# Highway output of a cross-covariance attention kernel written as T*max(h,0) - (T-1)*x

## The chip, the cores and the metric

The kernel runs on one core of a Trainium2 chip. The metric is the device time of one execution in microseconds (us), lower is better. Before the change the median of three runs is 414.38 us (414.25 to 415.24).

## What is computed

The inputs q, k and v have the shape (4, 6336, 256) in float32. The first half is a cross-covariance attention over channels, and its output x feeds a highway layer:

```python
qn = q / (norm(q, axis=1) + 1e-06)          # norm over the 6336 rows
kn = k / (norm(k, axis=1) + 1e-06)
a  = softmax(kn.T @ qn / tau)               # 256 x 256 per batch
x  = (v @ a).reshape(25344, 256)
H  = maximum(x @ w_h, 0)
T  = 1 / (1 + exp(-(x @ w_t + b_t)))
out = T * H + (1 - T) * x
```

## The kernel before

The four batches are worked one after another, and each has three stages. A row block has 128 rows (a subtile); a batch has 50 of them, the last with 64 rows, in groups of 16, 16, 16 and 2.

**Stage A** (L120 to L149) reads q and k and accumulates, over the 50 subtiles, six matmuls each into two PSUM banks (`sg`): k against q, and the two diagonal blocks that give the norms. **The middle** (L151 to L248) turns these into the softmax matrix `a`, transposes it (`at`), and multiplies it with w_h and w_t on TensorE. Its result `mr` holds three matrices side by side: `a` itself (columns 0 to C), a@w_h (C to 2C) and a@w_t (2C to 3C). So one pass over v gives x, h and the argument of the gate.

**Stage B** (L254 on) goes over the rows of v in pairs of subtiles, 24 full pairs and two single subtiles for each batch. For a pair, `emit_transpose` (L268) makes four matmuls against the identity into `vtps` (one PSUM buffer) and casts the result to f16 in SBUF as `vtsb` (four buffers). The cast is done by VectorE (DVE, L296) for even pairs and by ScalarE (ACT, L301) for odd ones. Transposes are written two pairs ahead (LOOKAHEAD). Then, for each subtile u of the pair, five matmuls follow in this order: `p3b` (L329), `p3a` (L336), `p3b`, `p3a`, and the bias into `p3b` (L343). A `p3a` bank holds x in columns 0 to C and h in columns C to 2C for one subtile, and there are three such banks. A `p3b` bank holds the gate's argument for both subtiles of a pair, and there are two.

The output of a pair is then made in five steps. ACT computes uu = sigmoid(-z) = 1 - T from `p3b` (L354) for the pair. For each subtile ACT computes hh = relu(h) from `p3a` (L366), and DVE computes dd = hh - x with x read from `p3a` (L370). GpSimd (POOL) computes pp = uu * dd for the pair (L378). DVE computes o = hh - pp into the output stage (L382). A `p3a` bank is free for TensorE when hh and dd of its subtile are done. The tiles uu, hh, dd and pp have four buffers each.

Loads of q, k and v are issued by POOL's queue (L401, L408), stores by the sync engine's queue (L418, L425), one store per 8 subtiles. A framework puts the instructions of each engine in an order, allots buffers and sets the waits; each engine then works strictly in that order.

Of the kernel before, what the change touches and what calls it, by code (L numbers as in the profile page):

```python
# [9 lines left out]
AluOp = mybir.AluOpType  # L10
Act = mybir.ActivationFunctionType
f32 = mybir.dt.float32
# [3 lines left out]
P = 128  # L16
# [3 lines left out]
def kernel(  # L20
# [11 lines left out]
    nc = tc.nc  # L32

    B, N, C = q.shape
# [7 lines left out]
    def rows_of(s):  # L42
        return last_rows if s == nsub - 1 else P
# [5 lines left out]
    while s < nsub:  # L49
# [7 lines left out]
    small_pool = ctx.enter_context(tc.tile_pool(name="small", bufs=4))  # L57
# [14 lines left out]
        out=wht[:, :, 0:C], in_=moe_w_h.rearrange("(kt jl) m -> jl kt m", kt=2)  # L72
    )
    nc.gpsimd.dma_start(
        out=wht[:, :, C : 2 * C], in_=moe_w_t.rearrange("(kt jl) m -> jl kt m", kt=2)
# [26 lines left out]
    def load_v(bb, gi):  # L102
        s0, ns = groups[gi]
        vt = stream_pool.tile([P, ns, C], f16, tag="v_in", bufs=3,
                              name=f"v{bb}_{gi}")
        _load_group(nc, vt, v[bb], s0, ns, rows_of)
        v_tiles[(bb, gi)] = vt
# [4 lines left out]
    for b in range(B):  # L112
# [7 lines left out]
        for gi, (s0, ns) in enumerate(groups):  # L120
            qt = q_tiles.pop((b, gi))
            kt_ = k_tiles.pop((b, gi))
            for si in range(ns):
                s_idx = s0 + si
                nr = rows_of(s_idx)
# [33 lines left out]
        for idx, (c, off) in enumerate(  # L159
# [3 lines left out]
                out=junk[:, idx, :],  # L163
                in0=ssb[:, c, off : off + P],
                scalar=0.0,
                in1=ident0,
                op0=AluOp.bypass,
                op1=AluOp.mult,
# [8 lines left out]
        for c in range(2):  # L177
            nc.vector.tensor_scalar(
                out=dcat[:, c, :],
                in0=ident0,  # L180
                scalar1=inv[:, 2 + c : 3 + c],
                scalar2=inv_tau,
                op0=AluOp.mult,
                op1=AluOp.mult,
# [7 lines left out]
        for c in range(2):  # L192
            nc.vector.scalar_tensor_tensor(
                out=t1[:, c, :],
                in0=ssb[:, c, 0:C],
                scalar=inv[:, c : c + 1],
                in1=cqbs,
                op0=AluOp.mult,
                op1=AluOp.mult,
# [5 lines left out]
            out=rs, in_=araw, axis=mybir.AxisListType.X, op=AluOp.add  # L205
# [3 lines left out]
        for c in range(2):  # L209
            nc.vector.tensor_scalar(  # L210
                out=mr[:, c, 0:C],
                in0=araw[:, c, :],
                scalar1=rinv[:, c : c + 1],
                scalar2=None,
                op0=AluOp.mult,
                op1=AluOp.bypass,
# [15 lines left out]
        for jk in range(2):  # L232
            nc.scalar.copy(
                out=at_sb[:, jk, :].rearrange("p (ic i) -> p ic i", ic=2),
                in_=atps[:, :, jk, :],
# [19 lines left out]
        for gi, (s0, ns) in enumerate(groups):  # L255
            si = 0
            while si < ns:
                pn = min(2, ns - si)
                if pn == 2 and rows_of(s0 + si) != rows_of(s0 + si + 1):
                    pn = 1  # L260
# [7 lines left out]
        def emit_transpose(pi):  # L268
            gi, s0, si, pn, nrows = pairs[pi]
            if si == 0:  # L270
                if gi + 1 < len(groups):
                    load_v(b, gi + 1)
                ostg_tiles[gi] = stream_pool.tile(
                    [P, groups[gi][1], C], f32, tag="o_out", name=f"o{b}_{gi}"
                )
            vt_in = v_tiles[(b, gi)]
            vtps = psum_pool.tile(
                [P, 2, 2, P], f32, tag="vtps", name=f"vtps{b}_{gi}_{si}"
            )
            pcnt = 0  # L280
            for u in range(pn):
                nr = nrows[u]
                for c in range(2):
                    nc.tensor.matmul(  # L284
                        vtps[:, u, c, 0:nr],
                        vt_in[0:nr, si + u, bass.ts(c, P)],
                        ident[0:nr, 0:nr],
                        start=(pcnt == 0),
                        stop=(pcnt == 2 * pn - 1),
                    )  # L290
                    pcnt += 1
            vt_sb = work_pool.tile(
                [P, 2, 2, P], f16, tag="vtsb", bufs=4, name=f"vtsb{b}_{gi}_{si}"
            )
            if pi % 2 == 0:
                nc.vector.tensor_copy(  # L296
                    out=vt_sb[:, 0:pn, :, 0 : nrows[0]],
                    in_=vtps[:, 0:pn, :, 0 : nrows[0]],
                )
            else:  # L300
                nc.scalar.copy(  # L301
                    out=vt_sb[:, 0:pn, :, 0 : nrows[0]],
                    in_=vtps[:, 0:pn, :, 0 : nrows[0]],
                )
            vtsb_tiles[pi] = vt_sb

        for pi in range(min(LOOKAHEAD, len(pairs))):
            emit_transpose(pi)

        for pi in range(len(pairs)):  # L310
            if pi + LOOKAHEAD < len(pairs):
                emit_transpose(pi + LOOKAHEAD)
            gi, s0, si, pn, nrows = pairs[pi]
            vt_sb = vtsb_tiles.pop(pi)
            ostg = ostg_tiles[gi]
            ns = groups[gi][1]
            p3b = psum_pool.tile(
                [P, 2, C], f32, tag="p3b", bufs=2, name=f"p3b_{b}_{gi}_{si}"
            )
            p3a = []  # L320
            for u in range(pn):
                nr = nrows[u]
                pa = psum_pool.tile(
                    [P, 2 * C], f32, tag="p3a", bufs=3,
                    name=f"p3a_{b}_{s0 + si + u}",
                )
                p3a.append(pa)
                for kt in range(2):
                    nc.tensor.matmul(  # L329
                        p3b[0:nr, u, :],  # L330
                        vt_sb[:, u, kt, 0:nr],
                        mr[:, kt, 2 * C : 3 * C],
                        start=(kt == 0 and u == 0),
                        stop=False,
                    )
                    nc.tensor.matmul(  # L336
                        pa[0:nr, :],
                        vt_sb[:, u, kt, 0:nr],
                        mr[:, kt, 0 : 2 * C],
                        start=(kt == 0),  # L340
                        stop=(kt == 1),
                    )
                nc.tensor.matmul(  # L343
                    p3b[0:nr, u, :],
                    ident[:, 0:nr],
                    btb,
                    start=False,
                    stop=(u == pn - 1),
                )

            nr0 = nrows[0]
            uu = small_pool.tile([P, 2, C], f32, tag="uu",
                                 name=f"uu{b}_{gi}_{si}")
            nc.scalar.activation(  # L354
                out=uu[0:nr0, 0:pn, :],
                in_=p3b[0:nr0, 0:pn, :],
                func=Act.Sigmoid,
                scale=-1.0,
            )
            hh = small_pool.tile([P, 2, C], f32, tag="hh",  # L360
                                 name=f"hh{b}_{gi}_{si}")
            dd = small_pool.tile([P, 2, C], f32, tag="dd",
                                 name=f"dd{b}_{gi}_{si}")
            for u in range(pn):
                nr = nrows[u]
                nc.scalar.activation(  # L366
                    out=hh[0:nr, u, :], in_=p3a[u][0:nr, C : 2 * C],
                    func=Act.Relu,
                )
                nc.vector.tensor_tensor(  # L370
                    out=dd[0:nr, u, :],
                    in0=hh[0:nr, u, :],
                    in1=p3a[u][0:nr, 0:C],
                    op=AluOp.subtract,
                )
            pp = small_pool.tile([P, 2, C], f32, tag="pp",
                                 name=f"pp{b}_{gi}_{si}")
            nc.gpsimd.tensor_tensor(  # L378
                out=pp[0:nr0, 0:pn, :], in0=uu[0:nr0, 0:pn, :],
                in1=dd[0:nr0, 0:pn, :], op=AluOp.mult,  # L380
            )
            nc.vector.tensor_tensor(  # L382
                out=ostg[0:nr0, si : si + pn, :], in0=hh[0:nr0, 0:pn, :],
                in1=pp[0:nr0, 0:pn, :], op=AluOp.subtract,
            )


            if si + pn >= ns:
                o0 = 0
                while o0 < ns:  # L390
                    on = min(OGS, ns - o0)
                    _store_group(nc, ob, ostg, s0, o0, on, rows_of)
                    o0 += on
                del ostg_tiles[gi]
                v_tiles.pop((b, gi))
# [36 lines left out]
_INS = ['q', 'k', 'v', 'tau', 'moe_w_h', 'moe_w_t', 'moe_b_t']  # L432
_OUTS = [((25344, 256), 'float32')]
#: Inputs that are plain numbers.
_NUMBERS = {'tau': 1.0}


# [26 lines left out]
```

## Time and profile before

| | |
|---|---|
| median of three runs | 414.38 us (414.25 to 415.24) |
| span of the profiled execution, first to last instruction | 412.4 us |
| TensorE (PE) matmul busy | 297.5 us, 72% |
| DVE busy | 208.9 us, 51% |
| ACT busy | 183.3 us, 44% |
| POOL busy | 189.2 us, 46% |
| chain that ended last, by engine | PE 24%, DMA 24%, DVE 23%, POOL 17%, issue 7%, ACT 4% |

The profile gives no other time for the profiled execution than its span; 2.0 us lie between that span and the median. The engines' shares are averages over the stages, and no engine is near 100%. The chain of waits is followed back from the last instruction, so its shares tell which work the end waited for. Busy times of matmuls overlap each other, so spacing between starts, not the sum of durations, tells what TensorE can do.

### The profile page before, as it was taken

The numbers are of one execution on the slowest core, as the hardware profiler recorded it, in microseconds if no ns is written. First come the engines' busy times: TensorE is split into PE (matmuls) and PEld (weight loads), VectorE is DVE, ScalarE is ACT, GpSimd is POOL, SyncE is SP. The second block draws the span as 40 slices with busy tenths as digits, with TensorE's granted clock in tenths as the row PEclk, the third lists the DMA queues.
The fourth block names the chain that finished last, engine by engine and source line by source line (L and its number), as shares of the span: only waits on it lengthen the run. The fifth ranks groups of instructions, "written<-read, shape, count | busy, mean of one in ns | idle before, by whom it ended". The sixth has DMA issues, their size and how long they took to land.

```text
span 412.4 us, 6770 instructions
## 1 busy us (share of the span) xinstructions
PE 297.5 (72%) x2637; PEld 212.1 (51%) x2637; DVE 208.9 (51%) x426; ACT 183.3 (44%) x407; POOL 189.2 (46%) x173
## 2 busy tenths in 40 slices
PE   0186839809877899968777999777778938776770
PEld 0176737506544698544445986444447815444440
DVE  0000103707876704497767232887766144786663
ACT  1000126605655306756555055566552166655561
POOL 9212322634646634555548441557366002754453
PEclk9999969957999999999999999999999968999996
DMA  7999999999962999999439999494329700433333
GB/s 95 198 199 197 198 198 199 197 233 188 195 193 70 217 245 198 197 222 241 124 103 173 238 205 198 94 209 138 109 67 215 163 0 0 113 102 103 103 102 121
DMA packets 103456, 65.57 MB, mean 159 GB/s; under 512 B 1537, under 2 KB 103425, under 8 KB 103425
## 3 DMA queue, kind: packets, MB, share of 16 engines
q0 software_dynamic: 77568, 39.20, 70.3%
q1 hardware_dynamic: 25856, 25.95, 20.6%
q8 instruction: 20, 0.33, 0.3%
q14 instruction: 12, 0.09, 0.1%
HBM read 78.38 MB, written 25.95 MB: 253 GB/s over the span
## 4 chain that ended last, share of the span: by engine, by line
PE 24%; DMA 24%; DVE 23%; POOL 17%; issue 7%; ACT 4%; POOLq 0%; DVEq 0%; ACTq 0%
POOL pp L378 15%; DVE o L382 14%; DMA k<-in_k_dram 14%; DVE dd L370 7%; PE p3a L336 7%; DMA v<-in_v_dram 6%; PE sg L129 5%; DMA q<-in_q_dram 4%; PE p3b L329 3%; PE sg L136 2%; PE sg L143 2%; PE vtps L284 2%; ACT hh L366 2%; PE p3b L343 1%; DVE vtsb L296 1%
## 5 line engine op out<-in xcount | busy, mean ns | idle before, releaser
L378 POOL TENSOR_TENSOR pp<-uu,dd 128x512 f32<-128x512 f32 (+1 forms) x104 | 131.4, 1273 | 144.0 <-DVE dd L370 64.8
L336 PE MATMUL p3a<-mr,vtsb 128*128 128x512 f16 (+1 forms) x400 | 134.7, 385 | 33.6 <-DVE dd L370 33.5
L382 DVE TENSOR_TENSOR o<-hh,pp 128x512 f32<-128x512 f32 (+1 forms) x104 | 94.4, 923 | 52.3 <-POOL pp L378 52.3
L366 ACT ACTIVATE hh<-p3a 128x256 f32<-128x256 f32 x200 | 76.1, 386 | 87.1 <-PE p3a L336 57.5
L129 PE MATMUL sg<-q,k 128*128 128x256 f16 (+1 forms) x400 | 94.7, 281 | 25.0 <-DMA k<-in_k_dram 24.1
L329 PE MATMUL p3b<-mr,vtsb 128*128 128x256 f16 (+1 forms) x400 | 100.3, 276 | 0.6 <-ACT uu L354 0.5
L370 DVE TENSOR_TENSOR dd<-hh,p3a 128x256 f32<-128x256 f32 x200 | 75.4, 413 | 29.2 <-ACT hh L366 29.0
L136 PE MATMUL sg<-k 128*128 128x128 f16 (+1 forms) x400 | 89.8, 225 | 0.0
L143 PE MATMUL sg<-q 128*128 128x128 f16 (+1 forms) x400 | 89.7, 224 | 0.0
L296 DVE CAST vtsb<-vtps 128x512 f16<-128x512 f32 (+1 forms) x52 | 34.5, 664 | 98.4 <-PE vtps L284 98.1
L284 PE MATMUL vtps<-ident,v 128*128 128x128 f16 (+1 forms) x400 | 41.1, 222 | 34.9 <-DVE vtsb L296 22.7
L336 PEld LDWEIGHTS <-vtsb 128*128 128x128 f16 (+1 forms) x400 | 39.3, 99 | 42.4 <-issue 18.9
L329 PEld LDWEIGHTS <-vtsb 128*128 128x128 f16 (+1 forms) x400 | 39.3, 99 | 42.2 <-issue 26.7
L354 ACT ACTIVATE uu<-p3b 128x512 f32<-128x512 f32 (+1 forms) x104 | 59.8, 579 | 0.1
L284 PEld LDWEIGHTS <-v 128*128 128x128 f16 (+1 forms) x400 | 30.8, 99 | 54.2 <-issue 32.6
L129 PEld LDWEIGHTS <-k 128*128 128x128 f16 (+1 forms) x400 | 40.2, 100 | 30.5 <-DMA k<-in_k_dram 29.9
L343 PE MATMUL p3b<-btb,ident 128*128 128x256 f16 x200 | 55.2, 276 | 0.0
L143 PEld LDWEIGHTS <-q 128*128 128x128 f16 (+1 forms) x400 | 40.2, 101 | 6.9 <-issue 1.1
L301 ACT CAST vtsb<-vtps 128x512 f16<-128x512 f32 (+1 forms) x52 | 29.3, 563 | 29.2 <-PE vtps L284 29.2
L153 ACT COPY ssb<-sg 128x512 f32<-128x512 f32 x8 | 4.3, 589 | 84.7 <-PE sg L143 84.7
L136 PEld LDWEIGHTS <-k 128*128 128x128 f16 (+1 forms) x400 | 40.2, 101 | 1.7 <-issue 1.4
L401 POOL DMA_DIRECT2D k<-in_k_dram x12 | 14.1, 1176 | 27.9 <-PE sg L143 23.5
(44 smaller groups left out, 123.2 us busy)
## 6 DMA issues: line engine op xcount, KB each, us to landing
out_dram<-o SPq DMA_DIRECT2D x24, 1024.0 KB, 5.4
q<-in_q_dram POOLq DMA_DIRECT2D x12, 1024.0 KB, 19.6
k<-in_k_dram POOLq DMA_DIRECT2D x12, 1024.0 KB, 17.4
v<-in_v_dram POOLq DMA_DIRECT2D x12, 1024.0 KB, 18.0
out_dram<-o SPq DMA_DIRECT2D x4, 128.0 KB, 9.6
q<-in_q_dram POOLq DMA_DIRECT2D x4, 64.0 KB, 23.1
k<-in_k_dram POOLq DMA_DIRECT2D x4, 64.0 KB, 22.6
v<-in_v_dram POOLq DMA_DIRECT2D x4, 64.0 KB, 4.5
```

What stands on the lines that cost most here:

```text
L129: nc.tensor.matmul(sg[c][:, 0:C], kt_[0:nr, si, bass.ts(c, P)], qt[0:nr, si, :], start=first, stop=False,)
L136: nc.tensor.matmul(sg[c][:, C : C + P], kt_[0:nr, si, bass.ts(c, P)], kt_[0:nr, si, bass.ts(c, P)], start=False, stop=False,)
L143: nc.tensor.matmul(sg[c][:, C + P : C + 2 * P], qt[0:nr, si, bass.ts(c, P)], qt[0:nr, si, bass.ts(c, P)], start=False, stop=last,)
L284: nc.tensor.matmul(vtps[:, u, c, 0:nr], vt_in[0:nr, si + u, bass.ts(c, P)], ident[0:nr, 0:nr], start=(pcnt == 0), stop=(pcnt == 2 * pn - 1),)
L329: nc.tensor.matmul(p3b[0:nr, u, :], vt_sb[:, u, kt, 0:nr], mr[:, kt, 2 * C : 3 * C], start=(kt == 0 and u == 0), stop=False,)
L336: nc.tensor.matmul(pa[0:nr, :], vt_sb[:, u, kt, 0:nr], mr[:, kt, 0 : 2 * C], start=(kt == 0), stop=(kt == 1),)
L343: nc.tensor.matmul(p3b[0:nr, u, :], ident[:, 0:nr], btb, start=False, stop=(u == pn - 1),)
L354: nc.scalar.activation(out=uu[0:nr0, 0:pn, :], in_=p3b[0:nr0, 0:pn, :], func=Act.Sigmoid, scale=-1.0,)
L366: nc.scalar.activation(out=hh[0:nr, u, :], in_=p3a[u][0:nr, C : 2 * C], func=Act.Relu,)
L370: nc.vector.tensor_tensor(out=dd[0:nr, u, :], in0=hh[0:nr, u, :], in1=p3a[u][0:nr, 0:C], op=AluOp.subtract,)
L378: nc.gpsimd.tensor_tensor(out=pp[0:nr0, 0:pn, :], in0=uu[0:nr0, 0:pn, :], in1=dd[0:nr0, 0:pn, :], op=AluOp.mult,)
L382: nc.vector.tensor_tensor(out=ostg[0:nr0, si : si + pn, :], in0=hh[0:nr0, 0:pn, :], in1=pp[0:nr0, 0:pn, :], op=AluOp.subtract,)
```

## The change

The gate is kept as T (`tt`, sigmoid without the sign). DVE makes two products per subtile with one instruction each: th = max(h, 0) * T and ux = (T - 1) * x, each reading one operand from the `p3a` bank and one from `tt`. POOL subtracts them into the output stage. ACT's relu, DVE's difference dd, POOL's product and DVE's final subtraction go. The cast of the transposed v goes to DVE for every fourth pair instead of every second.

```diff
-            if pi % 2 == 0:
+            if pi % 4 == 0:
                 nc.vector.tensor_copy(out=vt_sb[...], in_=vtps[...])
...
             nc.scalar.activation(
-                out=uu[0:nr0, 0:pn, :],
+                out=tt[0:nr0, 0:pn, :],
                 in_=p3b[0:nr0, 0:pn, :],
                 func=Act.Sigmoid,
-                scale=-1.0,
             )
             for u in range(pn):
                 nr = nrows[u]
-                nc.scalar.activation(
-                    out=hh[0:nr, u, :], in_=p3a[u][0:nr, C : 2 * C],
-                    func=Act.Relu,
-                )
-                nc.vector.tensor_tensor(
-                    out=dd[0:nr, u, :],
-                    in0=hh[0:nr, u, :],
-                    in1=p3a[u][0:nr, 0:C],
-                    op=AluOp.subtract,
-                )
-            nc.gpsimd.tensor_tensor(
-                out=pp[0:nr0, 0:pn, :], in0=uu[0:nr0, 0:pn, :],
-                in1=dd[0:nr0, 0:pn, :], op=AluOp.mult,
-            )
-            nc.vector.tensor_tensor(
-                out=ostg[0:nr0, si : si + pn, :], in0=hh[0:nr0, 0:pn, :],
-                in1=pp[0:nr0, 0:pn, :], op=AluOp.subtract,
-            )
+                nc.vector.scalar_tensor_tensor(
+                    out=th[0:nr, u, :],
+                    in0=p3a[u][0:nr, C : 2 * C],
+                    scalar=0.0,
+                    in1=tt[0:nr, u, :],
+                    op0=AluOp.max,
+                    op1=AluOp.mult,
+                )
+                nc.vector.scalar_tensor_tensor(
+                    out=ux[0:nr, u, :],
+                    in0=tt[0:nr, u, :],
+                    scalar=1.0,
+                    in1=p3a[u][0:nr, 0:C],
+                    op0=AluOp.subtract,
+                    op1=AluOp.mult,
+                )
+            nc.gpsimd.tensor_tensor(
+                out=ostg[0:nr0, si : si + pn, :], in0=th[0:nr0, 0:pn, :],
+                in1=ux[0:nr0, 0:pn, :], op=AluOp.subtract,
+            )
```

## Rows read from the trace of the kernel before

**Rows 1.** Span and mean granted TensorE clock of the core.
```profile
core 0: 412.4 us, clock 0.950
```

**Rows 2.** Stretches of 10 us: length, busy us by engine (count), granted clock, DMA share, GB/s.
```profile
80.00:90.00 10.00, 1.14 (x8) 0.51 (x7) 2.88 (x7) 1.57 (x4) 4.72 (x4) 0.70 1.34 230
...
380.00:390.00 10.00, 7.43 (x56) 4.78 (x56) 6.09 (x14) 5.81 (x13) 5.06 (x4) 1.00 0.32 108
```

**Rows 3.** Chain of waits, 383 to 389 us: start us, us, what.
```profile
383.15 1.27 POOL pp L378
384.45 0.69 DVE o L382
...
388.00 0.39 ACT hh L366
388.42 1.28 POOL pp L378
```

**Rows 4.** Timeline of POOL: pair 7 and pair 24 of batch 0, pairs 1 and 24 after.
```profile
96.93 1.58 POOL L378 TENSOR_TENSOR pp<-uu,dd 128x512 f32<-128x512 f32 x1 [11.01 <-ACT uu L354]
...
138.55 3.77 POOL L378 TENSOR_TENSOR pp<-uu,dd 128x512 f32<-128x512 f32 x3 [1.37 <-DVE dd L370]
...
169.26 1.27 POOL L378 TENSOR_TENSOR pp<-uu,dd 128x512 f32<-128x512 f32 x1 [2.76 <-ACT uu L354]
...
225.34 3.77 POOL L378 TENSOR_TENSOR pp<-uu,dd 128x512 f32<-128x512 f32 x3 [1.36 <-DVE dd L370]
...
256.22 1.26 POOL L378 TENSOR_TENSOR pp<-uu,dd 128x512 f32<-128x512 f32 x1 [11.82 <-ACT uu L354]
...
313.29 3.77 POOL L378 TENSOR_TENSOR pp<-uu,dd 128x512 f32<-128x512 f32 x3 [1.36 <-DVE dd L370]
...
345.41 1.26 POOL L378 TENSOR_TENSOR pp<-uu,dd 128x512 f32<-128x512 f32 x1 [28.35 <-ACT uu L354]
...
403.89 1.94 POOL L378 TENSOR_TENSOR pp<-uu,dd 128x512 f32<-128x512 f32 x2 [1.20 <-DVE dd L370]
```

**Rows 5.** Timeline of all engines, 385 to 389 us.
```profile
385.06 1.07 DVE L370 TENSOR_TENSOR dd<-hh,p3a 128x256 f32<-128x256 f32 x3
...
385.52 0.38 PE L336 MATMUL p3a<-mr,vtsb 128*128 128x512 f16 x1 [0.61 <-DVE dd L370]
...
386.06 0.27 PE L343 MATMUL p3b<-btb,ident 128*128 128x256 f16 x1
386.17 0.39 PE L284 MATMUL vtps<-ident,v 128*128 128x128 f16 x4
...
386.39 0.27 PE L329 MATMUL p3b<-mr,vtsb 128*128 128x256 f16 x1
...
387.86 0.41 DVE L370 TENSOR_TENSOR dd<-hh,p3a 128x256 f32<-128x256 f32 x1
...
388.19 0.68 DVE L296 CAST vtsb<-vtps 128x512 f16<-128x512 f32 x1
```

**Rows 6.** Timeline at the start of stage B, batch 3, ACT and DVE.
```profile
341.97 0.38 ACT L366 ACTIVATE hh<-p3a 128x256 f32<-128x256 f32 x1 [1.33 <-PE p3a L336]
...
342.39 0.42 DVE L370 TENSOR_TENSOR dd<-hh,p3a 128x256 f32<-128x256 f32 x1 [5.18 <-ACT hh L366]
```

**Rows 7.** Groups by line and shape: busy us, mean ns, idle before.
```profile
L354 ACT ACTIVATE uu<-p3b 128x512 f32<-128x512 f32 x96 | 56.8, 596 | 0.1
...
L301 ACT CAST vtsb<-vtps 128x512 f16<-128x512 f32 x48 | 28.2, 588 | 29.0 <-PE vtps L284 29.0
...
L162 DVE SCALAR_TENSOR_TENSOR junk<-ssb,ident 128x128 f32<-128x128 f32 x16 | 3.7, 285 | 0.0
L193 DVE SCALAR_TENSOR_TENSOR t<-ssb,inv,cqbs 128x256 f32<-128x256 f32 x8 | 3.5, 481 | 2.6 <-ACT cqbs L189 2.6
```

**Rows 8.** Instructions by tile (dd, o), 340 to 400 us: duration ns, min/median/max.
```profile
L370 DVE TENSOR_TENSOR dd<-hh,p3a x45: 404/414/422, 342.4 to 399.1; 128x256 f32<-128x256 f32 x45
L382 DVE TENSOR_TENSOR o<-hh,pp x21: 673/693/1740, 346.7 to 397.8; 128x512 f32<-128x512 f32 x21
```

More of the change, by code (lines that the diff above doesn't have):

```diff
@@ L351 @@
             nr0 = nrows[0]
-            uu = small_pool.tile([P, 2, C], f32, tag="uu",
-                                 name=f"uu{b}_{gi}_{si}")
+            tt = small_pool.tile([P, 2, C], f32, tag="tt",
+                                 name=f"tt{b}_{gi}_{si}")
             nc.scalar.activation(
-                out=uu[0:nr0, 0:pn, :],
+                out=tt[0:nr0, 0:pn, :],
                 in_=p3b[0:nr0, 0:pn, :],
                 func=Act.Sigmoid,
-                scale=-1.0,
             )
-            hh = small_pool.tile([P, 2, C], f32, tag="hh",
-                                 name=f"hh{b}_{gi}_{si}")
@@ L362 @@
-            dd = small_pool.tile([P, 2, C], f32, tag="dd",
-                                 name=f"dd{b}_{gi}_{si}")
+            th = small_pool.tile([P, 2, C], f32, tag="th",
+                                 name=f"th{b}_{gi}_{si}")
+            ux = small_pool.tile([P, 2, C], f32, tag="ux",
+                                 name=f"ux{b}_{gi}_{si}")
             for u in range(pn):
                 nr = nrows[u]
-                nc.scalar.activation(
-                    out=hh[0:nr, u, :], in_=p3a[u][0:nr, C : 2 * C],
-                    func=Act.Relu,
-                )
-                nc.vector.tensor_tensor(
-                    out=dd[0:nr, u, :],
-                    in0=hh[0:nr, u, :],
+                nc.vector.scalar_tensor_tensor(
[5 more added lines that the diff above has]
+                    op1=AluOp.mult,
+                )
+                nc.vector.scalar_tensor_tensor(
+                    out=ux[0:nr, u, :],
+                    in0=tt[0:nr, u, :],
+                    scalar=1.0,
@@ L373 @@
                     in1=p3a[u][0:nr, 0:C],
-                    op=AluOp.subtract,
-                )
-            pp = small_pool.tile([P, 2, C], f32, tag="pp",
-                                 name=f"pp{b}_{gi}_{si}")
+                    op0=AluOp.subtract,
+                    op1=AluOp.mult,
+                )
             nc.gpsimd.tensor_tensor(
-                out=pp[0:nr0, 0:pn, :], in0=uu[0:nr0, 0:pn, :],
-                in1=dd[0:nr0, 0:pn, :], op=AluOp.mult,
-            )
-            nc.vector.tensor_tensor(
-                out=ostg[0:nr0, si : si + pn, :], in0=hh[0:nr0, 0:pn, :],
-                in1=pp[0:nr0, 0:pn, :], op=AluOp.subtract,
+                out=ostg[0:nr0, si : si + pn, :], in0=th[0:nr0, 0:pn, :],
```

## Prediction

> **What bounds the kernel now.** I read the spans first, then the stretches of 10 us, then the chain of waits, then the timeline inside one period of it. The span is 412.4 us at a mean granted clock of 0.950 [rows 1]. The stretches show two regimes. Up to about 93 us the transfers hold the kernel: from 80 to 90 us TensorE works 1.14 us of 10 while the DMA moves 230 GB/s. In the regime behind it, from 380 to 390 us, no engine is full (TensorE 7.43, DVE 6.09, ACT 5.81, POOL 5.06 of 10), the DMA moves 108 GB/s, and the clock is at its upper level of 2.4 GHz [rows 2]. So stage B waits on itself there: it is a loop of latencies, and not an engine, that sets its pace.
>
> The chain shows the loop. From one pp on the chain to the next it is 388.42 - 383.15 = 5.27 us, and it advances two pairs [rows 3]. The reader is to see the order: POOL multiplies for 1.27 us, DVE's o comes 0.03 us behind it and lasts 0.69, the dd of the next pair stands behind o in DVE's queue, and only that dd frees the p3a bank for which TensorE waits (0.61 us idle, released by dd) [rows 5]. TensorE then works until ACT's hh at 388.00, and hh ends just ahead of the next pp [rows 3]. So POOL's product and DVE's last subtraction, 1.27 and 0.69 us, hold TensorE up once in two pairs because they are ahead of dd in DVE's queue.
>
> The pace over whole batches comes from the pp of the first and the 24th pair of each batch (pair 7 to 24 in batch 0, behind the stall for v). It is 41.62, 56.08, 57.07 and 58.48 us [rows 4], 213.25 us in all for 17 + 3 x 23 = 86 intervals: **2.48 us per pair**. What lies outside (stage A, the middle, the start up to 96.93 us) holds nothing that the change edits, except for the first six pairs of batch 0, which run ahead of a transfer anyway. I take it as unchanged.
>
> **The change, part by part.** *Removed from ACT:* two relus per pair. *Moved to ACT:* a cast of 0.59 us for every fourth pair [rows 7]. ACT was not the bound and ends with less work: free. *POOL:* one 128x512 operation of two SBUF operands stays one such operation, 1.27 us [rows 4]; a subtraction for a product, between the same price and nothing known otherwise, and I take the same. Its place changes: nothing on DVE waits for it any more, only the store does, and the buffers of th and ux (four pairs deep). Cover: 1.27 us of work, and now and then a load's issue, in a period over 2.2 us.
>
> *DVE:* dd twice and o once go, four products come. The o goes with its long cases, where it starts under POOL's product and lasts up to 1740 instead of 693 ns. The products have one operand in PSUM and one in SBUF, as dd has, and dd never lasts over 422 ns, beside POOL or not [rows 8]. The price of scalar_tensor_tensor with a PSUM operand is in no row. From below: dd, 0.41 us, with the next instruction 0.33 us behind its start (387.86 to 388.19) [rows 5]. From above: the same operation at 128x256, 0.481 us, but with its scalar read from a tile. The row nearest to it is L162, the same operation with its scalar in the instruction: 0.285 us at 128 columns [rows 7]. From 256 to 512 columns a DVE operation of this kind grows from 0.414 to 0.693 us [rows 8], 0.14 us per 128 columns, so 0.285 + 0.14 = **0.42 us**, next start after 0.34. DVE's work per pair is at most 4 x 0.42 + 0.68/4 = 1.85 us, below the period.
>
> *The wait that the change adds:* th needs T, and T needs the whole pair's p3b, whose last matmul is the bias of the second subtile. Before, the first subtile's bank needed only its own p3a, hh and dd. With three banks, the second subtile of pair n+1 takes the bank of the first subtile of pair n. That closes a new loop, worked out from one release of p3a to the next:
>
> - p3a granted to the start of the bias matmul: 385.52 to 386.06, 0.54 us; the bias itself 0.27 [rows 5]
> - TensorE to ACT: 0.05, an estimate from the other two handovers
> - sigmoid over the pair: 0.60 [rows 7]
> - ACT to DVE: 341.97 + 0.38 to 342.39, 0.04 [rows 6]
> - th of the first subtile to the start of ux: 0.34; ux: 0.42
> - DVE to TensorE: 385.06 + 0.41 to 385.52, 0.05 [rows 5]
>
> The sum is 2.31 us. Beside it TensorE needs, per pair, two subtiles of 0.54 + 0.11 + 0.11 = 0.76 and 0.22 for the transposes (386.17 to 386.39) [rows 5], 1.74 us: it hides in the loop. Queued behind th and ux on DVE are the second subtile's two products and every fourth cast. The second bank comes free 2 x 0.34 us later, 1.0 us ahead of the next round: free. The cast on DVE (0.68 us [rows 5]) can come between. Its transposes are issued at 0.65, right behind the bias, and last 0.39, so it would run from 1.09 to 1.77, while th could start at 1.50; 0.27 on one pair in four is 0.07. **New period: 2.38 us.**
>
> The gain is 86 x (2.48 - 2.38) = 8.6 us. At the end of the run DVE's last subtraction goes but POOL's queue of three operations stays; I count nothing. 412.4 - 8.6 = 403.8 us of span; with the 2.0 us between span and median, **405.8 us**. The unknown prices give the ends of this case: no cast in the way and DVE at 0.41 and 0.33 makes 2.29 us and a gain of 16.3 (398); products half the way to the dearer row below (0.45, next start after 0.37) make 2.44 us and leave 3.4 (411). The change trades a loop of 2.48 us for another of nearly that length, so large sums of removed work (two relus, an o) matter little.
>
> **The rivals.**
>
> *1. The products are dearer, and nothing changes.* With 0.481 us and 0.40 to the next start the loop is 2.31 + 0.06 + 0.06 + 0.07 = 2.50, the time 416; in between lies no change. For it: the only 128x256 row of this operation [rows 7]. Against it: the surplus goes well with the scalar read from a tile, which the new ones don't have. The Trainium skill (VectorE: DVE Perf Modes, sections "The DRAIN you can't avoid" and "Rules for kernel authors") speaks against the change here: VectorE flushes its pipe behind each operation, so one is to keep the number of operations low, and the same section lets an operation that isn't held start earlier. Taken strictly, ux would start a full 0.42 behind th, which makes 2.46 us and 413; the row with a start 0.33 behind a start [rows 5] says otherwise.
>
> *2. Slower: an order that puts something between the bias and th.* The engines work in a fixed order that I can't see for the changed kernel. ACT now casts three pairs in four. If such a cast stands ahead of the sigmoid and starts just before it is due, the loop pays up to 0.59 [rows 7] on three pairs of four, 0.44: 2.31 + 0.44 = 2.75, 86 x 0.27 = 23 us more, 438. The same comes about if the cast on DVE stands behind the four products and TensorE's next transposes wait for it in the one vtps buffer. It decides from 0.17 us per pair on (2.48 - 2.31). For it: casts and transposes wait for each other already, in the one buffer. Against it: the transposes stand between pairs [rows 5], so that their cast falls due after the sigmoid.
>
> *3. Faster: the stalls are filled.* TensorE has 2.38 - 1.74 = 0.64 us to spare per pair. If the order puts stage A matmuls of the next batch there, 3 batches x 24 pairs x 0.64 = 46 us at most could move; half of it gives 383. Against it: TensorE idles 0.61 at a time now and nothing is put there [rows 5].
>
> *4. It doesn't do what it says.* If POOL falls behind and its four buffers fill, th waits for POOL as o did. With 1.27 us in 2.38 I see no reason: 414 at a small chance.
>
> **How the numbers follow.** The forecast has 0.50, rival 1 has 0.17, rival 2 has 0.20, rival 3 has 0.10, rival 4 has 0.03. A measurement can tell 0.3%, 1.2 us, from no change. Faster takes the forecast, rival 3 and a quarter of rival 1: 0.64. No change takes half of rival 1 and rival 4: 0.12. Slower is rival 2 and the rest of rival 1: 0.24. The range goes from 388, which takes in the smaller fillings of rival 3, to 426, half the way of rival 2; the forecast's own range is 398 to 411.
>
> **What would show it.** Right: in stage B TensorE's p3a waits on DVE ux and on nothing else, once per pair; the chain runs sigmoid, th, ux, p3a with POOL nowhere but at the end; the distance of the pairs' sigmoids is near 2.38 us; the products last about 0.42. Wrong: products of 0.48 or more (rival 1); the sigmoid waits on a cast, or TensorE's transposes on DVE's cast (rival 2); stage A matmuls inside stage B (rival 3); th waiting on POOL (rival 4). The forecast falls if the period is under 2.2 or over 2.48.

## The result and the profile after

The change took the time from 414.31 us (median of 4 runs, 414.04 to 415.24) to **385.43 us** (4 runs, 384.06 to 385.58): a ratio of 0.929, with an interval of 0.9265 to 0.9319. The direction is the one forecast; the gain is 28.9 us where the sum gave 8.6, and the time lies 2.6 us below the range.

The page of the changed kernel: span, busy time of each engine, and the chain that ended last by engine.

```profile
span 382.2 us, 6609 instructions
...
PE 296.3 (78%) x2637; PEld 211.6 (55%) x2637; DVE 172.4 (45%) x498; ACT 133.2 (35%) x231; POOL 186.1 (49%) x173
...
PE 42%; DMA 39%; DVE 5%; ACT 4%; POOL 4%; issue 3%; POOLq 0%; DVEq 0%; ACTq 0%
```

DVE and POOL made up 40% of the chain before and make up 9% now; TensorE and the transfers hold 81%. The groups of the same page (busy us, mean ns of one, idle time before them and what ended it):

```profile
L381 POOL TENSOR_TENSOR o<-th,ux 128x512 f32<-128x512 f32 (+1 forms) x104 | 128.7, 1246 | 111.1 <-DVE ux L373 93.6
L336 PE MATMUL p3a<-mr,vtsb 128*128 128x512 f16 (+1 forms) x400 | 126.3, 386 | 1.0
...
L365 DVE SCALAR_TENSOR_TENSOR th<-p3a,tt 128x256 f32<-128x256 f32 x200 | 84.1, 421 | 41.1 <-ACT tt L354 24.6
...
L373 DVE SCALAR_TENSOR_TENSOR ux<-tt,p3a 128x256 f32<-128x256 f32 x200 | 82.1, 410 | 0.0
```

Two readings stand here. The products last 421 and 410 ns, as priced (0.42). And TensorE idles 1.0 us in the whole run ahead of p3a, although the forecast had it wait for ux once in every pair. So the forecast loop doesn't set the pace (short waits escape this column, as is shown below). The stretches of 10 us in batch 3's stage B, with the columns of [rows 2], say the same: TensorE is busy for 9.9 of 10 where it was for 7.43, at the same granted clock of 1.00, the upper level.

```profile
340.00:350.00 10.00, 9.93 (x77) 6.29 (x75) 8.62 (x24) 5.18 (x10) 7.21 (x7) 1.00 0.58 187
350.00:360.00 10.00, 9.89 (x75) 6.30 (x74) 8.21 (x24) 5.20 (x10) 7.38 (x6) 1.00 0.41 135
```

POOL's timeline gives the pace, as in [rows 4]. Shown are pairs 1 and 24 of batch 3, and before them two stretches of batches 0 and 1 that are new:

```profile
132.35 1.18 POOL L399 DMA_DIRECT2D q<-in_q_dram  x1
...
134.22 1.18 POOL L399 DMA_DIRECT2D k<-in_k_dram  x1
...
195.32 1.27 POOL L381 TENSOR_TENSOR o<-th,ux 128x512 f32<-128x512 f32 x1
208.53 1.29 POOL L381 TENSOR_TENSOR o<-th,ux 128x512 f32<-128x512 f32 x1 [11.94 <-DVE ux L373]
...
333.65 2.66 POOL L381 TENSOR_TENSOR o<-th,ux 128x512 f32<-128x512 f32 x2 [28.57 <-DVE ux L373]
...
374.93 2.64 POOL L381 TENSOR_TENSOR o<-th,ux 128x512 f32<-128x512 f32 x3 [0.49 <-DVE ux L373]
```

Batch 3 needs (374.93 - 333.65) / 23 = 1.79 us per pair, against 2.54 in the same batch before, and batch 2 needs 1.85. But between pairs 13 and 14 of batch 1 there are 13.2 us in which nothing is put out. The chain of waits names that gap and another one ahead of it (start us, us, what):

```profile
134.22 22.37 DMA k<-in_k_dram
156.64 0.39 PE sg L129
...
178.03 27.72 DMA v<-in_v_dram
205.79 0.61 PE vtps L284 x4
```

The first is a load of k for stage A of batch 2. It stands in POOL's queue at 134.22 here, while before it was issued at 79.86:

```profile
79.86 1.21 POOL L401 DMA_DIRECT2D k<-in_k_dram  x1 [0.75 <-PE sg L136]
```

The first load of q for batch 2 moved with it, from 102.89 to 132.35. Some of batch 2's stage A matmuls stand ahead of batch 1's stage B on TensorE, so TensorE waits for them. The second is a load of v for batch 1 that lands when stage B has already eaten what there was. It was issued at 177.98 before and at 178.03 here, and took 20.0 us to land before and 27.7 here. Put together from the starts of POOL's operation on each pair (also of those that the rows above hold together), the time went like this (us):

| stretch | before | after | difference |
|---|---|---|---|
| start to pair 7 of batch 0 | 96.9 | 99.2 | +2.3 |
| pairs 7 to 24, batch 0 | 41.6 | 31.3 | -10.4 |
| between batches 0 and 1 | 30.7 | 42.6 | +11.9 |
| pairs 1 to 24, batch 1 | 56.1 | 55.0 | -1.1 |
| pairs 1 to 24, batch 2 | 57.1 | 42.5 | -14.5 |
| pairs 1 to 24, batch 3 | 58.5 | 41.3 | -17.2 |
| the two other gaps and the end | 71.5 | 70.3 | -1.2 |

The differences add up to the 30.2 by which the spans differ. Stage B gained about 54 (10.4 + 14.5 + 17.2, and 12.4 in batch 1 if the stall of 13.2 is counted as one pair of 1.8), and about 23 came back as the two waits for transfers (11.9 and 11.4).

Why doesn't the loop set the pace? The order in which TensorE's instructions stand in the changed kernel shows it (this is a listing of the program and holds no times; the number behind p3b is the first subtile of its pair, the one behind p3a its subtile):

```
p3b_3_0_8     x2
p3a_3_6       x2
p3b_3_0_8     bias
p3b_3_0_8     x2
p3a_3_7       x2
p3b_3_0_8     bias
vtps          x3
p3a_3_8       x2
```

Here all gate matmuls and the closing bias of the pair of subtiles 8 and 9 stand ahead of that pair's own p3a matmuls, p3a_3_8 the first. That far ahead they are in 3 of the 24 full pairs of a batch. In most pairs the closing bias stands between the p3a of the first subtile and that of the second: it is ahead of the second subtile's p3a in 17, 16, 16 and 17 of 24 pairs (batches 0 to 3). In the kernel before it is in 4, 5, 5 and 4. With three banks, the second subtile's p3a is the one that takes the bank of the first subtile of the pair ahead. A sigmoid whose bias stands ahead of that p3a doesn't wait for that bank. It still waits for the p3a of its first subtile, whose bank comes from the pair before the last, so the loop closes once in two pairs there and not once in each. The framework made this of the edit; no line of the diff asks for it. In the timeline of batch 3 it looks like this (PEld is the loading of weights ahead of a matmul):

```profile
350.50 0.59 PE L336 MATMUL p3a<-mr,vtsb 128*128 128x512 f16 x2
...
350.58 0.60 ACT L354 ACTIVATE tt<-p3b 128x512 f32<-128x512 f32 x1 [0.74 <-ACT vtsb L301]
...
350.99 0.38 PE L329 MATMUL p3b<-mr,vtsb 128*128 128x256 f16 x2
...
351.21 0.27 PE L343 MATMUL p3b<-btb,ident 128*128 128x256 f16 x1
...
351.28 0.42 DVE L365 SCALAR_TENSOR_TENSOR th<-p3a,tt 128x256 f32<-128x256 f32 x1 [0.31 <-ACT tt L354]
351.32 0.59 PE L336 MATMUL p3a<-mr,vtsb 128*128 128x512 f16 x2
351.62 0.41 DVE L373 SCALAR_TENSOR_TENSOR ux<-tt,p3a 128x256 f32<-128x256 f32 x1
...
352.09 0.11 PEld L336 LDWEIGHTS <-vtsb 128*128 128x128 f16 x2 [0.24 <-DVE ux L373]
352.09 0.61 PE L336 MATMUL p3a<-mr,vtsb 128*128 128x512 f16 x2
...
352.54 0.27 PE L343 MATMUL p3b<-btb,ident 128*128 128x256 f16 x1
...
352.89 0.60 ACT L354 ACTIVATE tt<-p3b 128x512 f32<-128x512 f32 x1 [1.06 <-PE p3b L343]
...
354.20 0.60 ACT L354 ACTIVATE tt<-p3b 128x512 f32<-128x512 f32 x1 [0.24 <-ACT vtsb L301]
```

A sigmoid runs beside the p3a matmuls (350.58 and 350.50), and TensorE goes on from p3a to p3b, the bias and the next p3a (351.32) without a gap.

The later rows show a pair where the order was left as in the source, that of subtiles 24 and 25: its closing bias (352.54) stands behind its second p3a (352.09). There the forecast's loop is whole: sigmoid 350.58, th 351.28, ux 351.62, p3a 352.09, which takes the bank that this ux leaves at 352.03, bias 352.54, next sigmoid 352.89. That is 2.31 us, and the sigmoid of the next pair, whose bias stands ahead, follows after 1.31. Of pairs 2 to 24 of batch 3, six have their closing bias behind, and their sigmoid follows the one ahead after 2.31 to 2.45 us; those of the 17 others follow after 1.6 on average. The wait ahead of 352.09 is one of those that the idle column doesn't hold: the rows of matmuls overlap each other, and only the weight load shows it.

### The profile page after: what moved, and what is told of

Its sections match the earlier page's. It is cut to its first block, busy times and chain, and to the rows that moved or that the text cites. A ratio compares the mean times of both kernels' runs of the same rounds, so it can differ in the third digit from the quotient of the medians.

```text
span 382.2 us, 6609 instructions
## 1 busy us (share of the span) xinstructions
PE 296.3 (78%) x2637; PEld 211.6 (55%) x2637; DVE 172.4 (45%) x498; ACT 133.2 (35%) x231; POOL 186.1 (49%) x173
## 4 chain that ended last, share of the span: by engine, by line
PE 42%; DMA 39%; DVE 5%; ACT 4%; POOL 4%; issue 3%; POOLq 0%; DVEq 0%; ACTq 0%
DMA k<-in_k_dram 21%; PE p3a L336 19%; DMA v<-in_v_dram 14%; PE p3b L329 8%; DMA q<-in_q_dram 5%; PE p3b L343 4%; PE vtps L284 4%; PE sg L129 3%; ACT tt L354 3%; DVE th L365 2%; DVE ux L373 2%; PE sg L136 2%; PE sg L143 2%; POOL q L399 1%; POOL o L381 1%
## 5 line engine op out<-in xcount | busy, mean ns | idle before, releaser
L381 POOL TENSOR_TENSOR o<-th,ux 128x512 f32<-128x512 f32 (+1 forms) x104 | 128.7, 1246 | 111.1 <-DVE ux L373 93.6
L336 PE MATMUL p3a<-mr,vtsb 128*128 128x512 f16 (+1 forms) x400 | 126.3, 386 | 1.0
L365 DVE SCALAR_TENSOR_TENSOR th<-p3a,tt 128x256 f32<-128x256 f32 x200 | 84.1, 421 | 41.1 <-ACT tt L354 24.6
L354 ACT ACTIVATE tt<-p3b 128x512 f32<-128x512 f32 (+1 forms) x104 | 60.3, 581 | 101.5 <-PE p3b L343 87.8
L329 PE MATMUL p3b<-mr,vtsb 128*128 128x256 f16 (+1 forms) x400 | 87.0, 276 | 0.5 <-ACT tt L354 0.3
L373 DVE SCALAR_TENSOR_TENSOR ux<-tt,p3a 128x256 f32<-128x256 f32 x200 | 82.1, 410 | 0.0
L296 DVE CAST vtsb<-vtps 128x512 f16<-128x512 f32 (+1 forms) x28 | 18.2, 651 | 123.9 <-PE vtps L284 103.7
L284 PE MATMUL vtps<-ident,v 128*128 128x128 f16 (+1 forms) x400 | 45.2, 225 | 29.7 <-DMA v<-in_v_dram 25.4
L129 PEld LDWEIGHTS <-k 128*128 128x128 f16 (+1 forms) x400 | 40.6, 101 | 42.5 <-DMA k<-in_k_dram 41.2
L301 ACT CAST vtsb<-vtps 128x512 f16<-128x512 f32 (+1 forms) x76 | 43.1, 567 | 33.9 <-PE vtps L284 31.8
L343 PEld LDWEIGHTS <-ident 128*128 128x128 f16 x200 | 19.8, 99 | 13.0 <-issue 2.0
## 6 DMA issues: line engine op xcount, KB each, us to landing
out_dram<-o SPq DMA_DIRECT2D x4, 128.0 KB, 11.9
```

Source lines behind the costliest of these rows:

```text
L129: nc.tensor.matmul(sg[c][:, 0:C], kt_[0:nr, si, bass.ts(c, P)], qt[0:nr, si, :], start=first, stop=False,)
L284: nc.tensor.matmul(vtps[:, u, c, 0:nr], vt_in[0:nr, si + u, bass.ts(c, P)], ident[0:nr, 0:nr], start=(pcnt == 0), stop=(pcnt == 2 * pn - 1),)
L301: nc.scalar.copy(out=vt_sb[:, 0:pn, :, 0 : nrows[0]], in_=vtps[:, 0:pn, :, 0 : nrows[0]],)
L329: nc.tensor.matmul(p3b[0:nr, u, :], vt_sb[:, u, kt, 0:nr], mr[:, kt, 2 * C : 3 * C], start=(kt == 0 and u == 0), stop=False,)
L336: nc.tensor.matmul(pa[0:nr, :], vt_sb[:, u, kt, 0:nr], mr[:, kt, 0 : 2 * C], start=(kt == 0), stop=(kt == 1),)
L343: nc.tensor.matmul(p3b[0:nr, u, :], ident[:, 0:nr], btb, start=False, stop=(u == pn - 1),)
```

## The experiments

Three questions are left to the chip. Is TensorE's order the cause? What is each part of the change worth? Do transfers take back what stage B gains? All ratios are to the kernel before, whose median in the four batches of runs was 414.18 to 414.64.

### TensorE held to the source's order

An order without a semaphore is set between the stage B matmuls (transposes excepted), and the next batch's stage A (but its first group) is held behind the last pair, as it mostly stands anyway. The lines are shortened.

```diff
+        def in_order(mm):
+            if mm_prev:
+                tc.add_manual_dep(mm.ins, mm_prev[-1].ins.name, NoSync)
+            mm_prev.append(mm)
...
-                    nc.tensor.matmul(p3b[0:nr, u, :], ...)
+                    in_order(nc.tensor.matmul(p3b[0:nr, u, :], ...))
...
+        if gi > 0 and last_b:
+            tc.add_manual_dep(mm.ins, last_b[-1].ins.name, NoSync)
```

> The changed kernel with TensorE's matmuls of stage B pinned to the order of the source (for each subtile p3b, p3a, p3b, p3a, bias), and the next batch's stage A, from its second group on, pinned behind the last pair. Theory O (what my sum missed is the order on TensorE: the gate's matmuls of the next pair stand ahead of the wait for a p3a bank, so the sigmoid is no longer in the loop): with the source's order my loop is back, 2.3 to 2.45 us per pair in batch 3, and the whole takes 402 to 415 us. Theory B (the banks come free early enough whatever the order): 1.8 us per pair and 383 to 388 us.

Measured: **438.11 us** (437.62 to 439.76), ratio 1.059 (1.0561 to 1.0619): slower than before the change, and above what was expected, in time as in pace. Its timeline in batch 3 (start us, us, engine, line, what; idle before and what ended it):

```profile
391.07 0.59 ACT L324 CAST vtsb<-vtps 128x512 f16<-128x512 f32 x1 [1.70 <-PE p3a L359]
...
391.55 0.60 ACT L377 ACTIVATE tt<-p3b 128x512 f32<-128x512 f32 x1
...
392.26 0.42 DVE L388 SCALAR_TENSOR_TENSOR th<-p3a,tt 128x256 f32<-128x256 f32 x1 [1.37 <-ACT tt L377]
392.60 0.41 DVE L396 SCALAR_TENSOR_TENSOR ux<-tt,p3a 128x256 f32<-128x256 f32 x1
...
393.06 0.38 PE L359 MATMUL p3a<-mr,vtsb 128*128 128x512 f16 x1 [0.88 <-DVE ux L396]
...
396.53 1.29 POOL L404 TENSOR_TENSOR o<-th,ux 128x512 f32<-128x512 f32 x1 [1.50 <-DVE ux L396]
...
398.63 0.38 PE L359 MATMUL p3a<-mr,vtsb 128*128 128x512 f16 x1 [0.88 <-DVE ux L396]
...
399.32 1.28 POOL L404 TENSOR_TENSOR o<-th,ux 128x512 f32<-128x512 f32 x1 [1.49 <-DVE ux L396]
399.37 0.69 DVE L319 CAST vtsb<-vtps 128x512 f16<-128x512 f32 x1
...
399.52 0.60 ACT L377 ACTIVATE tt<-p3b 128x512 f32<-128x512 f32 x1 [1.80 <-issue]
...
400.22 0.43 DVE L388 SCALAR_TENSOR_TENSOR th<-p3a,tt 128x256 f32<-128x256 f32 x1 [0.17 <-ACT tt L377]
...
401.03 0.38 PE L359 MATMUL p3a<-mr,vtsb 128*128 128x512 f16 x1 [0.50 <-DVE ux L396]
...
401.72 1.29 POOL L404 TENSOR_TENSOR o<-th,ux 128x512 f32<-128x512 f32 x1 [1.12 <-DVE ux L396]
```

This is the forecast's loop: sigmoid, th, ux, then p3a, which waits for ux. In the pair whose cast is DVE's, it goes round in 401.03 - 398.63 = 2.40 us (and o follows o in 401.72 - 399.32 = 2.40). The sum had 2.31 for a round with no cast in the way, and 0.27 more where DVE's cast comes between. Here that cast costs nothing: it ends at 400.06, ahead of th at 400.22. In a pair with a cast on ACT the cast starts just before the sigmoid is due, as rival 2 had it, and the distance of the o is 399.32 - 396.53 = 2.79, 0.39 more. Over pairs 1 to 24 of batch 3 that makes 2.67 us per pair. So under the order that the forecast assumed, the forecast's loop and rival 2 hold together. That the time is rival 2's 438 to the microsecond is luck: that rival had 2.75 us per pair, and 7.8 us of the difference to the kernel before lie in the start up to pair 7 of batch 0 (104.76 for 96.93).

### The same order, with stage A free

The kernel above without its last two lines.

> The same pin of stage B's matmuls, but stage A of the next batch free: the framework then places about 200 of its 300 matmuls of a batch in the gaps of stage B. Theory O: stage B slower than in the changed kernel, 2.3 to 2.6 us per pair in batch 3, which has no next batch and so nothing to put in; batches 0 to 2 longer, their stage A shorter, the whole 385 to 400 us. Theory B: 1.8 us per pair in batch 3, and the whole 375 to 388.

Measured: **394.38 us** (393.79 to 396.22), ratio 0.953 (0.9504 to 0.9565). The pace is the same 2.67 us in batch 3, where there is no next batch, a little above the expected 2.3 to 2.6. But the framework placed 214, 226 and 187 stage A matmuls of later batches (a batch has 300) in the idle time of the stage B of batches 0, 1 and 2, and the gaps between batches shrink from 31 to 33 us to 18.8, 13.3 and 14.0. This is rival 3: it is real, and it is worth 44 us here. It isn't what the changed kernel does, whose gaps did not shrink.

### The other order, with the same pins

Only the order differs from the first experiment: the next pair's p3b matmuls (four and two biases) stand ahead of this pair's p3a, in every pair. The pins are those shown there.

```diff
+            if pi + 1 < len(pairs):
+                emit_gate(pi + 1)
+            p3b = p3b_tiles.pop(pi)
...
             for u in range(pn):
...
-                    nc.tensor.matmul(p3b[0:nr, u, :], ...)
                     nc.tensor.matmul(pa[0:nr, :], ...)
```

> The changed kernel with the same pins as in the program-order run (stage A of the next batch behind the last pair from its second group on, a fixed order of stage B's matmuls on TensorE), but the order is: the six gate matmuls of the next pair, then the p3a matmuls of this pair. It differs from that run in the order alone. Theory O: 1.75 to 1.9 us per pair in batch 3 against 2.67 there, and 380 to 392 us against 438. Theory B (the pins themselves, not the order, cost the time): 2.4 to 2.7 us per pair and 410 to 440.

Measured: **368.16 us** (367.57 to 369.43), ratio 0.8885 (0.885 to 0.892). The order alone is worth 438.11 - 368.16 = 70 us, more than was expected (380 to 392). Batch 3 needs 1.72 us per pair, batch 2 1.75. One stretch of each kernel's batch 3 (columns of [rows 2]), first the source's order, then the gate ahead:

```profile
390.00:400.00 10.00, 7.08 (x51) 4.56 (x51) 5.76 (x16) 3.73 (x7) 4.54 (x4) 1.00 0.31 105
```

```profile
330.00:340.00 10.00, 9.97 (x81) 6.62 (x79) 8.35 (x24) 6.01 (x11) 7.22 (x6) 1.00 0.34 113
```

TensorE is full in the second, and from 330 to 345 us the chain of waits of that kernel has TensorE alone but for 0.4%. Here th and ux come right behind the p3a, and a bank is held for 1.5 to 1.9 us, from the start of its p3a to the end of its ux (subtiles 10 to 45 of batch 3). A stall for v of 15.2 us is left in batch 1.

### The order in the kernel before

The gate ahead, on the kernel before, with no other edit.

> The kernel before, its arithmetic untouched, with the gate's six matmuls of the next pair put ahead of the p3a matmuls of this pair. If the gain of the change is the order on TensorE alone, this has most of it: 385 to 395 us. If it is that DVE no longer waits for POOL (theory P), the loop pp, o, dd, p3a, hh has no sigmoid in it and stays: 405 to 416 us, with DVE's o still waiting on POOL in the chain.

Measured: **424.60 us** (423.47 to 424.79), ratio 1.025 (1.0227 to 1.0275). This is slower than the kernel before and above what was expected. The loop of before has no gain from the order (2.51 us per pair in batches 1 and 2 and 2.63 in batch 3, for 2.44, 2.48 and 2.54); POOL is 26% and DVE 19% of its chain. What stands in the way there is pp ahead of o ahead of dd, and an earlier sigmoid shortens none of these. So the order by itself is not the gain: it counts with the new arithmetic, where th and ux need the sigmoid. Why it costs 10 us here was not tried.

### The product on DVE, the subtraction on POOL

The kernel before with its two last operations on each other's engines, so that DVE waits on POOL no more, and nothing else is changed.

```diff
-            nc.gpsimd.tensor_tensor(out=pp[...], ..., op=AluOp.mult)
+            nc.vector.tensor_tensor(out=pp[...], ..., op=AluOp.mult)
-            nc.vector.tensor_tensor(out=ostg[...], ..., op=AluOp.subtract)
+            nc.gpsimd.tensor_tensor(out=ostg[...], ..., op=AluOp.subtract)
```

> The kernel before with POOL and DVE changing places: the product pp on DVE, the last subtraction on POOL; relu stays on ACT, the casts stay halved. It takes away the wait of DVE on POOL and nothing else. Theory P: the period falls to DVE's own work, 2 x 0.33 + 0.6 to 0.9 + 0.3, so 1.8 to 2.1 us per pair in batch 3, and the whole takes 380 to 398 us. Rival: pp has two operands in SBUF and is held while POOL's own operation runs (o lasted up to 1.74 us in the kernel before), so DVE is full and the period stays at 2.4 or more: 408 to 420 us.

Measured: **392.28 us** (391.27 to 394.82), ratio 0.947 (0.9442 to 0.9494): 22 of the 29 us, with relu and dd still there. DVE's timeline in batch 3:

```profile
363.31 1.13 DVE L378 TENSOR_TENSOR pp<-uu,dd 128x512 f32<-128x512 f32 x1
364.36 0.74 DVE L370 TENSOR_TENSOR dd<-hh,p3a 128x256 f32<-128x256 f32 x2
365.02 0.68 DVE L296 CAST vtsb<-vtps 128x512 f16<-128x512 f32 x1
365.62 0.74 DVE L378 TENSOR_TENSOR pp<-uu,dd 128x512 f32<-128x512 f32 x1
366.29 0.74 DVE L370 TENSOR_TENSOR dd<-hh,p3a 128x256 f32<-128x256 f32 x2
367.15 1.13 DVE L378 TENSOR_TENSOR pp<-uu,dd 128x512 f32<-128x512 f32 x1
```

Two pairs take 367.15 - 363.31 = 3.84 us, 1.92 per pair, and DVE is packed; over batch 3 it is 1.95. The first gap between batches is 42.2 us, about as long as in the changed kernel, and the first q and k of batch 2 stand late here too, at 137.07 and 138.25. TensorE's order stayed near the source's (3 of 24 pairs with the gate ahead), which costs nothing here: dd doesn't need the sigmoid, so the sigmoid isn't between a bank's matmuls and its release. The rest of the change, with T in the product, puts it there, and the new order takes it out again.

### The subtraction on DVE

The changed kernel with its last subtraction moved from POOL to DVE (one word of the diff: gpsimd to vector).

> The changed kernel with the final subtraction back on DVE, so POOL only issues loads. Theory P (what counts is that DVE waits for nobody; then the busiest engine sets the pace): DVE has 4 x 0.33 + 0.6 + 0.15 = 2.1 us per pair and is the bound, 2.05 to 2.25 us per pair in batch 3; the framework puts about 148 stage A matmuls of each next batch into stage B, which gives some of it back: 388 to 402 us in all. Rival (the gain came from a shorter way from the gate to the output, and POOL's place in it doesn't matter): 1.8 us per pair and 383 to 388.

Measured: **376.48 us** (374.75 to 377.38), ratio 0.910 (0.9065 to 0.9127). This was a miss: it is 9 us faster than the change, not slower. Stage B is slower, as expected: 2.05 us per pair in batch 3 and 2.18 in batch 2, against 1.79 and 1.85. But the framework put 148 of a batch's stage A matmuls into it, and the three gaps between batches are 21.4, 20.2 and 21.5 us in place of 42.6, 31.8 and 31.2. With POOL free, the first k and q of batch 2 are issued at 97.55 and 98.68. The subtraction by tile, durations in ns (least, median, most):

```profile
L381 DVE TENSOR_TENSOR o<-th,ux x25: 408/677/679, 320.9 to 368.0; 128x512 f32<-128x512 f32 x23, 128x256 f32<-128x256 f32 x1, 64x256 f32<-64x256 f32 x1
```

It never lasts over 679 ns, where the same shape reached 1740 beside POOL's product [rows 8]; here POOL computes nothing in stage B.

### The relu kept, the casts as before

The changed kernel with ACT's two relus per pair put back, whose result nothing reads:

```diff
+                nc.scalar.activation(out=hh[0:nr, u, :],
+                    in_=p3a[u][0:nr, C : 2 * C], func=Act.Relu)
```

> The changed kernel with the two relus on ACT kept as extra work that nobody reads (0.56 to 0.77 us of ACT per pair, and each bank is free only when its relu is done too). Theory T (stage B is now TensorE's own 1.8 us per pair): no change, 383 to 389 us. Rival (the removed relus made room on ACT for the sigmoid): 1.95 us per pair or more, 392 to 402.

and the changed kernel with the cast on DVE for every second pair again:

```diff
-            if pi % 4 == 0:
+            if pi % 2 == 0:
```

> The changed kernel with the casts divided as before, every second one on DVE. Theory T: DVE has 4 x 0.33 + 0.3 = 1.65 us per pair, under TensorE's 1.8: 383 to 390 us. Rival (DVE near its limit lets products wait behind casts, so TensorE waits for banks): 1.9 us per pair or more, 391 to 400.

Measured: 380.98 us (377.13 to 382.52), ratio 0.918 (0.9127 to 0.924), and **374.26 us** (372.2 to 374.77), ratio 0.903 (0.899 to 0.9061). In stage B neither part is worth anything that shows: batch 3 needs 1.79 us per pair with the relus and 1.75 with the old casts. (The closing bias is ahead there in 18 and 23 of 24 pairs. With 0, 17 and 24, in the pinned run, the changed kernel and the gate-ahead run, it was 2.67, 1.79 and 1.72.) Both kernels come out below what was expected, and faster than the change, for another reason. Their first loads for batch 2 stand in POOL's queue at 77.08 (q) and 101.57 (k) with the relus, and with the old casts at 101.45 (q) and here:

```profile
80.11 1.19 POOL L399 DMA_DIRECT2D k<-in_k_dram  x1
```

Before the change they stood at 102.89 and 79.86, in the changed kernel at 132.35 and 134.22. The gap between batches 0 and 1 is 33.7 and 31.9 us, not 42.6. So the 12 us that the wait for k cost came from the place of two loads in a queue, which each of these small edits shifts back. The stall for v in batch 1 is another matter: it is there in both, 12.4 and 13.2 us from one pair to the next.

### The loads of v ahead of the next q and k

The changed kernel; all groups of a batch's v are asked for ahead of the next batch's q and k, with six buffers for v instead of three.

```diff
-                tag="v_in", bufs=3,
+                tag="v_in", bufs=6,
...
+        for gi in range(1, len(groups)):
+            load_v(b, gi)
         if b + 1 < B:
             load_qk(b + 1)
...
-                if gi + 1 < len(groups):
-                    load_v(b, gi + 1)
```

> The changed kernel with the remaining loads of v of a batch issued ahead of the loads of q and k for the next batch (six buffers of v instead of three). Theory D (the changed kernel lost about 13 us of its gain to transfers that it now waits for: v at 196 to 206 us in batch 1, k at 134 to 156 us, beside the stall at 80 to 95 that was there before): both stalls for v go, 360 to 375 us. Rival (the DMA is saturated up to there, so the wait only moves to q and k of the next stage A): 380 to 388.

Measured: **365.89 us** (365.36 to 367.05), ratio 0.884 (0.8808 to 0.8865). No pair of a batch waits for v any more, and all four batches run at 1.81 to 1.85 us per pair. The kernel's page, in 40 slices of 9.1 us: the DMA engines' busy share in tenths, and GB/s.

```profile
DMA  7999999999999999999999899998864400033554
GB/s 86 198 198 199 197 198 197 199 198 216 241 250 249 248 235 198 198 198 197 231 247 275 172 219 216 198 173 108 257 200 142 139 2 0 0 118 115 168 180 137
```

From the second slice to the 27th, some 9 to 246 us, the DMA engines are 90% busy or more in all slices but one. From these rows I read that transfers set the first half, and TensorE the second; the chain has 27% DMA and 52% TensorE.

### Parts together

Three kernels join edits whose diffs stand above. The first has the old casts and the loads of v first. The second has the subtraction on DVE and v first; the third is the first one with the gate ahead in every pair.

> The changed kernel with the casts halved and the loads of v first. If the two gains (385.4 to 374.3, and to 365.9) were different waits for transfers, they add up: 352 to 358 us. If both are the same transfers told differently, 363 to 368.

> The changed kernel with the final subtraction on DVE, POOL free for the loads, and the loads of v first. Theory D (behind the first v stall the loads set the pace of the first half, so a slower stage B costs nothing there): 362 to 370 us. Rival (DVE's 2.1 us per pair are now the bound everywhere): 372 to 382.

> The changed kernel with the gate of the next pair ahead (a fixed order of stage B's matmuls, stage A left free), the casts halved and the loads of v first. If the first half is now set by the loads (363.6 us with the last two), the fixed order adds nothing: 360 to 367 us. If stage B's own pace still counts, 352 to 359.

Measured: old casts and v first, **363.64 us** (363.02 to 365.24), ratio 0.878 (0.8741 to 0.8815); the subtraction on DVE and v first, 366.58 us (366.14 to 366.76), ratio 0.884 (0.8809 to 0.8879); old casts, v first and the gate ahead in every pair, **363.61 us** (five runs, 362.57 to 364.61), ratio 0.878 (0.8758 to 0.8801). The gains don't add: once v comes first, the old casts are worth 2 us and not 11, and a fixed order adds nothing. That it adds nothing doesn't show that the first half waits for bytes: the first kernel has the closing bias ahead in 23 of 24 pairs by itself and needs 1.75 to 1.88 us per pair, the third 1.76 to 1.84, so there was little left to gain. The two at 363.6 beat both kernels, and the changed one by 22 us.

## Why the prediction was right and wrong

**What bounds the kernel before** was right. With DVE's wait on POOL taken out and little else changed, 22 of the 29 us come (392.28), and the order alone brings none (424.60).

**The prices** were right: the products at 421 and 410 ns for 0.42, with ux 0.34 us behind th (351.28 and 351.62), so rival 1 (0.481) falls. POOL's subtraction lasts 1.29 us for 1.27 and nothing in stage B waits on it, so rival 4 falls. The removed relus are worth nothing, as costed.

**The new loop** was right as a mechanism and nearly in size, but for another program. It is there in the pairs whose closing bias the changed kernel leaves behind (2.31 to 2.45 us), and in every pair of the run that is held to it. That run's 2.40 and the sum's 2.38 agree in part by luck: the cast on DVE, 0.07 of the sum, cost nothing, and the handovers cost 0.09 more than priced (from the sigmoid to th 0.10 for 0.04, from the bias to the sigmoid 0.08 for 0.05). Even there the period would have been 2.67 and the time 438.11, since the casts on ACT stand ahead of the sigmoid. So the direction came out by luck too: in the order that the sum takes, the change makes the kernel slower. Rival 2 had 0.59 at most in each such pair, and 0.39 was measured. That rival got 0.20 on the argument that "the transposes stand between pairs". In that run they stand inside a pair, behind the first p3b of its second subtile and four pairs ahead, and the cast waits for a vtsb buffer that a p3a of the present pair frees (at 391.07, released by p3a), just ahead of the sigmoid.

**The step that failed** is the sum from "p3a granted to the start of the bias matmul" to "DVE to TensorE". It takes TensorE's order from the source, with the closing bias behind the pair's own p3a, so that the loop closes once in every pair. In the changed kernel the closing bias stands ahead of the second subtile's p3a in 16 or 17 of 24 pairs, where the loop closes once in two. The other pairs of batch 3 still take 2.31 to 2.45 us, these 1.6 on average, and together they come to 1.79. Where the gate is ahead in every pair, a bank is held for 1.9 us at most; three banks then serve one subtile per 0.65 us, and TensorE needs about 0.87 for one. The term that I had "hide in the loop", TensorE's 1.74 us per pair, became the bound: 1.72 and 1.75 were measured with the gate ahead everywhere, 1.79 and 1.85 in the changed kernel, where TensorE is 99% busy, and 86 x (2.48 - 1.74) = 64 us would have been its sum. That the order is the cause is shown by the pair of runs that differ in it alone, 438.11 and 368.16. I had written that the engines' order couldn't be seen for the changed kernel, and used that for a slower rival only. The same doubt had a faster side, p3b ahead of p3a, and none of the rivals had it. Rival 3, idle time filled with stage A, happens in other kernels here (394.38, 376.48) but not in this one.

**What lies outside stage B** ("I take it as unchanged") failed as well, the other way. Stage B eats v 0.7 us per pair sooner, and the loads behind it don't come sooner: the stall for v in batch 1 cost 11 us, and the first q and k of batch 2 put later in POOL's queue cost 12. Taken off the result by that table, they leave some 362 us. That v ahead of q and k, with six buffers, brings 19.5 us back is shown; why the framework moved the loads of q and k for this edit and not for its neighbours stays open.

## What to carry to other kernels

A loop summed from the trace of before holds only for the order that it was read in. Where a framework orders the instructions, ask of each link whether it could be issued earlier, price the loop with that link taken out, and put the engine's own need under it as the floor. A stage that gets faster eats its inputs sooner, so look up in POOL's or SP's queue where its loads stand; and compare small variants of an edit before you judge its parts, since the place of two loads moved some 11 us here.

## What was not expected of the hardware

A cast ahead of the sigmoid did not cost its full length. The sigmoid starts 0.48 us behind the start of a cast of 0.59 (391.07 and 391.55), and the loop pays 0.39, since the cast itself starts 0.09 us before the sigmoid is due. And the plain subtraction on DVE is shorter than on POOL (0.68 against 1.29 us) and is never held when POOL has no arithmetic beside it; in the kernel before, the three long cases of [rows 8] (1739 to 1740 ns) are the only ones that run beside POOL's product, for 1.19 us each. That it is POOL's arithmetic which holds them was not tried by itself.
